# Multiplying half of the columns of the self-mirrored slots in a first dense layer, and computing the rest from sums and differences

## The chip, the cores and the metric

The kernel runs on one core of one Trainium2 chip. The metric is the device time of one execution, in microseconds; lower is better. Every time below is a median of several executions, with the lowest and highest in brackets. All executions that are compared were at a mean granted TensorE clock of 0.991 to 0.996 of full speed.

## The reference

```python
x: (8, 3008, 256)                      # fp32
X = fft(fft(x, axis=1), axis=2).real   # over the sequence, then over the width
x2 = X.reshape(24064, 256)
h = x2 @ w_in                          # w_in: 256 x 2048
g = h * clip(h + 3, 0, 6) / 6
return g @ w_out                       # w_out: 2048 x 256, fp32
```

## The kernel before

The transform over the sequence is done as 47 x 64: a token has the index k1 (47 values) and k2 (64 values). Batches go in 4 pairs. Of each pair there are 12 chunks of 4 slots; a slot is one batch with one k1 and all 64 k2, so a chunk has 256 columns. A chunk takes 8 steps, 384 in all. Because the input is real, the token at (k1, k2) and its mirror at (-k1, -k2) share their products: the first layer computes an even part `u` and an odd part `v`, a one-row correction gives `s`, and the two tokens are `s + v` and `s - v`. A slot with k1 = 0 is its own mirror. Such slots are the last two of the last chunk of each pair.

This is one step's first layer and activation (`ns` is 3 and `nm` is 2 in the last chunk, else both are 4; asserts and other cases cut):

```python
def mlp1(ch, fc):
    u = ps_h.tile([P, 2, KC, N2], F32, tag="uv")   # PSUM, one bank; u and v share 3 buffers
    v = ps_h.tile([P, 2, KC, N2], F32, tag="uv")
    for blk, ps in ((0, u), (1, v)):
        for i in range(2):
            matmul(ps[:, i], W1[r, blk, f*P:(f+1)*P], q[r, blk, of:of+KC])
    for i in range(2):                              # s = u + qn * WN, to SBUF
        vector.scalar_tensor_tensor(s[:, i], qn[...], WN[:, f:f+1], u[:, i], mult, add)
    vector.tensor_tensor(u[:, :, 0:ns], s[:, :, 0:ns], v[:, :, 0:ns], add)
    relu(t[:, 0, :, 0:ns], u[:, :, 0:ns], 1/6)      # ScalarE
    if ch.last:                                     # the negated sum
        vector.scalar_tensor_tensor(u[:, :, 3], s[:, :, 3], -1.0, v[:, :, 3], mult, subtract)
        relu(t[:, 0, :, 3], u[:, :, 3], -1/6)
    vector.tensor_tensor(v[:, :, 0:nm], v[:, :, 0:nm], s[:, :, 0:nm], subtract)
    relu(t[:, 1, :, 0:nm], v[:, :, 0:nm], -1/6)
    gate(a[:, 0, :, 0:ns], t[:, 0, :, 0:ns], u[:, :, 0:ns])   # VectorE: min(t, 1) * u
    if ch.last:
        gate(a[:, 1, :, 2], t[:, 0, :, 3], u[:, :, 3])
    for i in ...:
        gate(a[:, 1, i, 0:nm, ::-1], t[:, 1, i, 0:nm], v[:, i, 0:nm])
```

The steps run in this order. The first layer is two steps ahead of the second, GpSimd forms sums for the second layer one step ahead, and in the first three steps of a chunk the chunk before it is finished: GpSimd recombines it in step 0 and VectorE transposes it in steps 1 and 2.

```python
for s, (p, ck, fc) in enumerate(steps):
    if s + 2 < len(steps): mlp1(*chunk(s + 2))
    if s + 1 < len(steps): combine(*chunk(s + 1))     # GpSimd
    if prev and fc < 3:
        finish(prev) if fc == 0 else store(prev, fc - 1)
    mlp2(*chunk(s))            # 14 MATMULs: 7 products, Strassen-like
    ...
```

## Time and profile before

| | before |
|---|---|
| median of 3 runs | 2004.63 us (2003.18 to 2004.73) |
| span of the profiled run, granted clock | 2001.0 us, 0.993 |
| TensorE work of a step of the last chunk, by the prediction's sum | 4.01 us |
| what a step there takes, without and with transposes (pair 1) | 4.12 us, 4.68 and 4.69 us |
| first to seventh second-layer call of a last chunk, pairs 0, 1, 2 | 26.59, 25.94, 25.96 us |
| first to sixth, pair 3 | 21.82 us |

The lines of the profile are shown in the prediction. The last two rows of the table are the measure that I call "the stretch". It runs from the start of the first second-layer call of a last chunk to the start of the seventh; in pair 3, which has no next pair to begin, to the start of the sixth. It holds the five steps that the prediction calls bound by VectorE.

### The profile page before, as it was taken

The page shows a single profiled execution, that of the slowest core. Times are in us where ns is not written, and L with a number is a line of the kernel's source. Part 1 is how long each engine was busy: PE and PEld are TensorE (multiplying, and loading weights), DVE is VectorE, ACT ScalarE, POOL GpSimd, SP SyncE. Part 2 cuts the span into 40 slices and gives each one's busy share as a digit, 9 for nine tenths or more (in the row PEclk, how much of TensorE's full clock was granted, in tenths as well). Part 3 has the DMA queues.
Part 4 walks back from the last instruction along what each step waited for, and adds up shares of the span by engine and source line. Part 5 has one row for each costly group of instructions (what it writes and reads, how often), then busy time and mean ns, then how long its engine had stood idle before and what let it go on. Part 6 is the DMA issues. An engine that isn't in the chain of part 4 may idle for free.

```text
span 2001.0 us, 28370 instructions
## 1 busy us (share of the span) xinstructions
PE 1965.6 (98%) x9178; PEld 1691.6 (85%) x9178; DVE 1440.1 (72%) x2711; ACT 700.3 (35%) x1196; POOL 1416.2 (71%) x1608
## 2 busy tenths in 40 slices
PE   8899999999999999999999999999999999999997
PEld 5588888888888888888888888888888888888886
DVE  5677767776777677776777767777678777777776
ACT  6533333333333333333333333333333333333322
POOL 3277778776777787777658877778666667667664
PEclk9899999999999999999999999999999999999999
DMA  9512212211111122110201221212110101101100
GB/s 296 143 28 58 51 40 50 57 36 35 29 34 51 41 52 59 47 51 25 50 17 30 70 57 39 51 44 52 35 27 20 27 17 26 33 12 27 27 12 19
DMA packets 158665, 93.54 MB, mean 47 GB/s; under 512 B 130635, under 2 KB 143467, under 8 KB 158518
## 3 DMA queue, kind: packets, MB, share of 16 engines
q1 hardware_dynamic: 148310, 57.99, 12.0%
q0 software_dynamic: 9600, 33.59, 6.0%
q8 instruction: 75, 1.23, 0.2%
q14 instruction: 72, 0.59, 0.1%
q10 hardware_dynamic: 608, 0.13, 0.0%
HBM read 54.32 MB, written 37.33 MB: 46 GB/s over the span
## 4 chain that ended last, share of the span: by engine, by line
PE 93%; DVE 3%; ACT 1%; issue 1%; POOL 0%; DVEq 0%; POOLq 0%; ACTq 0%
PE acc L382 55%; PE v L326 16%; PE u L326 16%; PE ps L280 2%; PE ps L226 2%; DVE a L358 1%; ACT t L355 0%; DVE u L339 0%; DVE s L331 0%; DVE o L440 0%; ACT PM L498 0%; PE wps L563 0%; DVE v L345 0%; DVE u L342 0%; ACT q L282 0%
## 5 line engine op out<-in xcount | busy, mean ns | idle before, releaser
L372 POOL TENSOR_TENSOR c<-a 128x512 f32<-128x512 f32 (+1 forms) x383 | 478.2, 1249 | 452.3 <-PE acc L382 358.3
L382 PE MATMUL acc<-c,G 128*128 128x256 f32 (+1 forms) x3072 | 712.0, 375 | 0.0
L355 ACT ACTIVATE t<-u,half 128x512 f32<-128x512 f32 (+2 forms) x416 | 272.5, 655 | 1105.7 <-DVE u L339 1094.1
L382 PEld LDWEIGHTS acc<-c,G 128*128 128x128 f32 x3072 | 577.5, 190 | 72.8
L331 DVE SCALAR_TENSOR_TENSOR s<-qn,WN,u 128x256 f32<-128x256 f32 x768 | 334.2, 476 | 352.8 <-PE u L326 352.4
L382 PE MATMUL acc<-a,G 128*128 128x256 f32 (+1 forms) x2304 | 551.7, 375 | 0.0
L382 PEld LDWEIGHTS acc<-a,G 128*128 128x128 f32 x2304 | 434.9, 190 | 57.7
L326 PE MATMUL v<-q,W 127*128 127x256 f32 x1536 | 398.6, 381 | 7.6 <-DVE a L358 7.6
L326 PE MATMUL u<-q,W 128*128 128x256 f32 x1536 | 395.4, 380 | 1.8 <-DVE a L358 1.5
L326 PEld LDWEIGHTS u<-q,W 128*128 128x128 f32 x1536 | 287.8, 190 | 59.7 <-issue 15.6
L326 PEld LDWEIGHTS v<-q,W 127*128 127x128 f32 x1536 | 290.2, 190 | 55.7 <-issue 8.2
L358 DVE SCALAR_TENSOR_TENSOR a<-t,u 128x512 f32<-128x512 f32 (+2 forms) x416 | 265.9, 646 | 96.0 <-ACT t L355 90.0
L372 POOL TENSOR_TENSOR c<-c,a 128x256 f32<-128x256 f32 (+1 forms) x383 | 274.7, 717 | 30.0
L372 POOL TENSOR_TENSOR c<-a,c 128x256 f32<-128x256 f32 (+1 forms) x383 | 274.5, 717 | 30.0
L339 DVE TENSOR_TENSOR u<-s,v 128x512 f32<-128x512 f32 (+1 forms) x384 | 263.1, 685 | 42.1 <-PE v L326 1.6
L355 ACT ACTIVATE t<-v,half 128x512 f32<-128x512 f32 (+1 forms) x384 | 257.1, 670 | 5.8 <-DVE v L345 4.4
L345 DVE TENSOR_TENSOR v<-v,s 128x512 f32<-128x512 f32 (+1 forms) x384 | 257.7, 671 | 1.1
L358 DVE SCALAR_TENSOR_TENSOR a<-t,v 128x512 f32<-128x512 f32 (+1 forms) x416 | 254.9, 619 | 0.5
L372 POOL TENSOR_TENSOR r<-w,e 128x256 f32<-128x256 f32 (+1 forms) x94 | 90.8, 987 | 3.7
L390 ACT ACTIVATE e<-acc 128x512 f32<-128x512 f32 (+2 forms) x190 | 86.3, 544 | 2.8 <-PE acc L382 2.7
L440 DVE STREAM_TRANSPOSE o<-r 128x256 f32<-128x256 f32 (+1 forms) x192 | 72.5, 415 | 0.4
L238 ACT COPY z<-ps 96x512 f32<-96x512 f32 x64 | 37.2, 581 | 82.8 <-PE ps L226 62.5
(91 smaller groups left out, 755.7 us busy)
## 6 DMA issues: line engine op xcount, KB each, us to landing
out_dram<-o SPq DMA_DIRECT2D x732, 32.0 KB
zd<-z SPq DMA_DIRECT2D x32, 384.0 KB
g<-zd SPq DMA_DIRECT2D x48, 256.0 KB
xt<-in_x_dram POOLq DMA_DIRECT2D x21, 384.0 KB, 4.0
qn<-qd SPq DMA_DIRECT2D x23, 256.0 KB
st<-in_moe_w_in_dram POOLq DMA_DIRECT2D x8, 512.0 KB, 11.1
st<-in_moe_w_out_dram POOLq DMA_DIRECT2D x8, 512.0 KB, 5.0
xt<-in_x_dram POOLq DMA_DIRECT2D x7, 376.0 KB, 3.9
```

Source lines behind the costliest of these rows:

```text
L226: nc.tensor.matmul(ps[0:PZ], F[0:PR, 0:PZ], y[:, 2 * i:2 * i + 2, :], start=True, stop=True)
L280: nc.tensor.matmul(ps[:, blk, 2 * u:2 * u + 2], g[:, kk, blk * (P + 1):blk * (P + 1) + P], T[:, :, gr, blk, kk], start=True, stop=True)
L326: nc.tensor.matmul(ps[:, i], W1[r, blk, f * P:(f + 1) * P], q[r, blk, of:of + KC], start=True, stop=True)
L331: nc.vector.scalar_tensor_tensor(s[:, i].rearrange("p k n -> p (k n)"), qn[:, of * N2:(of + KC) * N2], WN[:, f:f + 1], u[:, i].rearrange(" ...
L339: nc.vector.tensor_tensor(u[:, :, 0:ns], s[:, :, 0:ns], v[:, :, 0:ns], op=AL.add)
L345: nc.vector.tensor_tensor(v[:, :, 0:nm], v[:, :, 0:nm], s[:, :, 0:nm], op=AL.subtract)
L355: nc.scalar.activation(t, h, AF.Relu, bias=half[:], scale=scale)
L358: nc.vector.scalar_tensor_tensor(dst, t, 1.0, h, op0=AL.min, op1=AL.mult)
L372: (eng or nc.gpsimd).tensor_tensor(out, in0, in1, op=AL.add)
L382: nc.tensor.matmul(ch.acc[i // 2][:, i % 2, 0:ch.n], G[:, i, fc, :], mv, start=(fc == 0 and i % 2 == 0), stop=(fc == NF - 1), skip_group_c ...
L390: nc.scalar.mul(ch.e[:, k:i + 1, 0:ch.n], ch.acc[i // 2][:, 0:i + 1 - k, 0:ch.n], 1.0 / WS)
L440: nc.vector.transpose(o[:, 0:n // DH, h], ch.r[:, m, h, 0:n].rearrange("p (j i) -> p j i", i=DH))
```

## The change

In a slot with k1 = 0, the even part is the same at k2 and at 64 - k2, and the odd part has the opposite sign. So products for k2 = 0 to 32 are enough (`NH` = 33): the last chunk has 128 + 66 = 194 columns to multiply in place of 256. The tokens k2 = 33 to 63 come from the same products with the signs exchanged. The intent is to save TensorE about a quarter of the first layer in 32 of the 384 steps. VectorE gets more and smaller instructions for it. The diff, cut to the first layer and the activation (the second transform stage also skips the 31 columns of both slots):

```diff
     def mlp1(ch, fc):
-                nc.tensor.matmul(ps[:, i], W1[r, blk, f * P:(f + 1) * P], q[r, blk, of:of + KC],
+                nc.tensor.matmul(ps[:, i, 0:nq], W1[r, blk, f * P:(f + 1) * P], q[r, blk, of:of + nq],
                                  start=True, stop=True)
...
+    def activate_last(a, t, s, u, v):
+        n, e2, e3 = 2 * N2, 2 * N2 + NH, 2 * N2 + 2 * NH      # 128, 161, 194
+        m = NH - 2                                            # 31
+        two, three = slice(n + 1, e2 - 1), slice(e2 + 1, e3 - 1)
+        mine, minus = slice(e2, e2 + m), slice(e2 + m, e3 + m)
+        nc.vector.tensor_tensor(u[:, :, 0:e2], s[:, :, 0:e2], v[:, :, 0:e2], op=AL.add)
+        nc.vector.tensor_tensor(u[:, :, mine], s[:, :, two], v[:, :, two], op=AL.subtract)
+        nc.vector.scalar_tensor_tensor(u[:, :, minus], s[:, :, e2:e3], -1.0, v[:, :, e2:e3],
+                                       op0=AL.mult, op1=AL.subtract)
+        relu(t[:, 0, :, 0:e2 + m], u[:, :, 0:e2 + m], 1.0 / 6.0)
+        relu(t[:, 0, :, minus], u[:, :, minus], -1.0 / 6.0)
+        nc.vector.tensor_tensor(v[:, :, 0:e3 - 1], v[:, :, 0:e3 - 1], s[:, :, 0:e3 - 1], op=AL.subtract)
+        relu(t[:, 1, :, 0:e3 - 1], v[:, :, 0:e3 - 1], -1.0 / 6.0)
+        back = slice(3 * N2 - 1, e2 - 1, -1)
+        gate(a[:, 0, :, 0:e2], t[:, 0, :, 0:e2], u[:, :, 0:e2])
+        gate(a[:, 0, :, back], t[:, 0, :, mine], u[:, :, mine])
+        gate(a[:, 1, :, n:e2], t[:, 0, :, minus], u[:, :, minus])
+        for i in range(2):
+            ...  gate(rev[:, :, ::-1], tk, vk)                # 2 x 128 elements, reversed
+        gate(a[:, 1, :, back], t[:, 1, :, three], v[:, :, three])
```

Besides the width, the order changes: the negated sum now comes before the first activation.

More of the change, by code (lines that the diff above doesn't have):

```diff
@@ L82 @@
     TB = KC * N2
+    NH = N2 // 2 + 1
     NG = NCK // 2
@@ L272, in stage2 @@
         if i == 0:
-            pr.q[gr] = qpool.tile([P, 2, 2 * KC, N2], F32, tag="q", name="q")
+            pr.q[gr] = qpool.tile([P, 2, 2 * TB], F32, tag="q", name="q")
         g = pr.g[gr]
-        ps = bank([P, 2, 4, N2], "ps2")
+        ps = bank([P, 2, TB], "ps2")
         for u in range(2):
             kk = 2 * i + u
+            nk = NH if (gr, kk) == (NG - 1, 2 * KK - 1) else N2
+            n = u * P + 2 * nk
             for blk in range(2):
-                nc.tensor.matmul(ps[:, blk, 2 * u:2 * u + 2], g[:, kk, blk * (P + 1):blk * (P + 1) + P],
-                                 T[:, :, gr, blk, kk], start=True, stop=True)
-        nc.scalar.copy(pr.q[gr][:, :, 4 * i:4 * i + 4, :], ps[:])
+                nc.tensor.matmul(ps[:, blk, u * P:n].rearrange("p (b k) -> p b k", b=2),
+                                 g[:, kk, blk * (P + 1):blk * (P + 1) + P],
+                                 T[:, :, gr, blk, kk, 0:nk], start=True, stop=True)
+        nc.scalar.copy(pr.q[gr][:, :, i * TB:i * TB + n], ps[:, :, 0:n])
     def spread(pr, gr):
@@ L293, in spread @@
         else:
+            n = 2 * TB if gr < NG - 1 else 3 * P + 2 * NH
             qd = dpool.tile([1, 2 * TB], F32, tag="qd", name="qd")
-            nc.sync.dma_start(out=qd[:], in_=pr.q[gr][P - 1:P, 1].rearrange("p k n -> p (k n)"))
-            nc.sync.dma_start(out=pr.qn[gr][:], in_=qd[:].to_broadcast([P, 2 * TB]))
+            nc.sync.dma_start(out=qd[:, 0:n], in_=pr.q[gr][P - 1:P, 1, 0:n])
+            nc.sync.dma_start(out=pr.qn[gr][:, 0:n], in_=qd[:, 0:n].to_broadcast([P, n]))
         del pr.g[gr]
@@ L306, in __init__ @@
             self.ns = 3 if self.last else KC
-            self.nm = 2 if self.last else KC
             self.n = self.ns * N2
+            self.nq = P + 2 * NH if self.last else TB
             self.a, self.c, self.acc = {}, {}, {}
@@ L316, in mlp1 @@
     def mlp1(ch, fc):
-        gr, of = ch.ck // 2, ch.ck % 2 * KC
+        gr, of, nq = ch.ck // 2, ch.ck % 2 * TB, ch.nq
         q, qn = ch.pr.q[gr], ch.pr.qn[gr]
-        u = ps_h.tile([P, 2, KC, N2], F32, tag="uv", name="u")
-        v = ps_h.tile([P, 2, KC, N2], F32, tag="uv", name="v")
+        u = ps_h.tile([P, 2, TB], F32, tag="uv", name="u")
+        v = ps_h.tile([P, 2, TB], F32, tag="uv", name="v")
         for blk, ps in ((0, u), (1, v)):
@@ L325, in mlp1 @@
                 f = fc + i * NF
-                nc.tensor.matmul(ps[:, i], W1[r, blk, f * P:(f + 1) * P], q[r, blk, of:of + KC],
+                nc.tensor.matmul(ps[:, i, 0:nq], W1[r, blk, f * P:(f + 1) * P], q[r, blk, of:of + nq],
                                  start=True, stop=True)
-        s = spool.tile([P, 2, KC, N2], F32, tag="s", name="s")
+        s = spool.tile([P, 2, TB], F32, tag="s", name="s")
         for i in range(2):
             f = fc + i * NF
-            nc.vector.scalar_tensor_tensor(
-                s[:, i].rearrange("p k n -> p (k n)"), qn[:, of * N2:(of + KC) * N2], WN[:, f:f + 1],
-                u[:, i].rearrange("p k n -> p (k n)"), op0=AL.mult, op1=AL.add)
@@ L336, in mlp1 @@
-        ns, nm = ch.ns, ch.nm
-        a = apool.tile([P, 2, 2, KC, N2], F32, tag="a", name="a")
-        t = spool.tile([P, 2, 2, KC, N2], F32, tag="t", name="t")
-        nc.vector.tensor_tensor(u[:, :, 0:ns], s[:, :, 0:ns], v[:, :, 0:ns], op=AL.add)
-        relu(t[:, 0, :, 0:ns], u[:, :, 0:ns], 1.0 / 6.0)
-        if ch.last:
-            nc.vector.scalar_tensor_tensor(u[:, :, 3], s[:, :, 3], -1.0, v[:, :, 3],
-                                           op0=AL.mult, op1=AL.subtract)
-            relu(t[:, 0, :, 3], u[:, :, 3], -1.0 / 6.0)
@@ L345, in mlp1 @@
-        nc.vector.tensor_tensor(v[:, :, 0:nm], v[:, :, 0:nm], s[:, :, 0:nm], op=AL.subtract)
-        relu(t[:, 1, :, 0:nm], v[:, :, 0:nm], -1.0 / 6.0)
-        gate(a[:, 0, :, 0:ns], t[:, 0, :, 0:ns], u[:, :, 0:ns])
-        if ch.last:
-            gate(a[:, 1, :, 2], t[:, 0, :, 3], u[:, :, 3])
-        for i in (slice(0, 2),) if nm == KC else (0, 1):
-            gate(a[:, 1, i, 0:nm, ::-1], t[:, 1, i, 0:nm], v[:, i, 0:nm])
-        ch.a[fc] = a
+            nc.vector.scalar_tensor_tensor(s[:, i, 0:nq], qn[:, of:of + nq], WN[:, f:f + 1], u[:, i, 0:nq],
+                                           op0=AL.mult, op1=AL.add)
@@ new lines, in mlp1 @@
+        a = apool.tile([P, 2, 2, TB], F32, tag="a", name="a")
+        t = spool.tile([P, 2, 2, TB], F32, tag="t", name="t")
+        ch.a[fc] = a
+        if ch.last:
+            activate_last(a, t, s, u, v)
+            return
+        nc.vector.tensor_tensor(u[:], s[:], v[:], op=AL.add)
+        relu(t[:, 0], u[:], 1.0 / 6.0)
+        nc.vector.tensor_tensor(v[:], v[:], s[:], op=AL.subtract)
+        relu(t[:, 1], v[:], -1.0 / 6.0)
+        gate(a[:, 0], t[:, 0], u[:])
+        rev, tk, vk = (m.rearrange("p i (k n) -> p (i k) n", n=N2) for m in (a[:, 1], t[:, 1], v[:]))
@@ new lines, in mlp1 @@
+        gate(rev[:, :, ::-1], tk, vk)
+    def activate_last(a, t, s, u, v):
[16 more added lines that the diff above has]
+        for i in range(2):
+            rev, tk, vk = (x.rearrange("p (k n) -> p k n", n=N2) for x in (a[:, 1, i, 0:n], t[:, 1, i, 0:n], v[:, i, 0:n]))
+            gate(rev[:, :, ::-1], tk, vk)
+        gate(a[:, 1, :, back], t[:, 1, :, three], v[:, :, three])
@@ L360, in combine @@
     def combine(ch, fc):
-        a = ch.a[fc][:].rearrange("p m f k n -> p (m f) (k n)")[:, :, 0:ch.n]
+        a = ch.a[fc][:].rearrange("p m f n -> p (m f) n")[:, :, 0:ch.n]
         c = cpool.tile([P, 4, TB], F32, tag="c", name="c")
@@ L374, in mlp2 @@
     def mlp2(ch, fc):
-        a = ch.a.pop(fc)[:].rearrange("p m f k n -> p (m f) (k n)")[:, :, 0:ch.n]
+        a = ch.a.pop(fc)[:].rearrange("p m f n -> p (m f) n")[:, :, 0:ch.n]
         c = ch.c.pop(fc)
```

## The prediction

> **What bounds the kernel now.** I read the page from the top: busy shares, then the chain that ended last, then the groups by shape, and last the timeline of one stretch. The page says:
>
> ```profile
> PE 1965.6 (98%) x9178; PEld 1691.6 (85%) x9178; DVE 1440.1 (72%) x2711; ACT 700.3 (35%) x1196; POOL 1416.2 (71%) x1608
> ...
> PE 93%; DVE 3%; ACT 1%; issue 1%; POOL 0%; DVEq 0%; POOLq 0%; ACTq 0%
> ```
>
> TensorE is the bound nearly everywhere: 93% of the chain. But the change touches only the last of the 12 chunks of each of the 4 pairs of batches, 8 steps each, 32 of 384 steps, so the average does not answer; that chunk has to be read by itself. A step is one first-layer call (8 MATMULs, two for each of four products), the activation on VectorE and ScalarE, the sums on GpSimd, and one second-layer call (14 MATMULs). The first-layer call runs two steps ahead. TensorE in pair 1's last chunk, timeline (start, duration):
>
> ```profile
> 1036.19 1.10 PE L326 MATMUL v<-q,W 127*128 127x256 f32 x4 [0.44 <-DVE a L358]
> 1037.13 1.14 PE L382 MATMUL acc<-a,G 128*128 128x192 f32 x6
> 1038.10 1.46 PE L382 MATMUL acc<-c,G 128*128 128x192 f32 x8
> 1039.40 1.03 PE L326 MATMUL u<-q,W 128*128 128x256 f32 x4
> 1040.31 1.10 PE L326 MATMUL v<-q,W 127*128 127x256 f32 x4
> ```
>
> The step lasts 1040.31 - 1036.19 = 4.12 us. TensorE's own work is less: the chain has 14 second-layer MATMULs of 192 columns in 2.28 us (162.8 ns each) and elsewhere 14 of 256 in 3.02 us (216 ns), so a step needs 8 x 216 + 2.28 = 4.01 us. In front of the v product it waits for the gate (the line `a`, L358). VectorE, then ScalarE, in the same step:
>
> ```profile
> 1036.36 0.86 DVE L331 SCALAR_TENSOR_TENSOR s<-qn,WN,u 128x256 f32<-128x256 f32 x2
> 1037.33 0.56 DVE L339 TENSOR_TENSOR u<-s,v 128x384 f32<-128x384 f32 x1
> 1038.60 0.30 DVE L342 SCALAR_TENSOR_TENSOR u<-s,v 128x128 f32<-128x128 f32 x1 [0.71 <-ACT t L355]
> 1038.93 0.43 DVE L345 TENSOR_TENSOR v<-v,s 128x256 f32<-128x256 f32 x1
> 1039.41 0.75 DVE L358 SCALAR_TENSOR_TENSOR a<-t,u 128x384 f32<-128x384 f32 x2
> 1040.08 0.48 DVE L358 SCALAR_TENSOR_TENSOR a<-t,v 128x128 f32<-128x128 f32 x2
> 1040.47 0.48 DVE L331 SCALAR_TENSOR_TENSOR s<-qn,WN,u 128x256 f32<-128x256 f32 x1
> ```
>
> ```profile
> 1037.98 0.58 ACT L355 ACTIVATE t<-u,half 128x384 f32<-128x384 f32 x1 [2.09 <-DVE u L339]
> 1038.93 0.37 ACT L355 ACTIVATE t<-u,half 128x128 f32<-128x128 f32 x1 [0.36 <-DVE u L342]
> 1039.46 0.47 ACT L355 ACTIVATE t<-v,half 128x256 f32<-128x256 f32 x1 [0.16 <-DVE v L345]
> ```
>
> VectorE starts the next step's `s` 4.11 us after this one and has no gap above 0.11 us in between but the 0.71 us in which L342 waits for ScalarE. So this chunk is bound by the serial run of VectorE, wait included. A second loop is as long: u and v share three PSUM buffers, so the v product of a step starts only when the u gates of the step before are done (1040.16, the product starts 1040.31). In two steps of each last chunk VectorE also transposes the chunk before (0.76 us for two), and these last 4.68 and 4.69 us (v product to v product, 1026.82, 1031.50, 1036.19). From the first second-layer call of pair 1's last chunk (1019.42) to the seventh (1045.36) pass 25.94 us; TensorE alone would need 6 x 4.01 = 24.06.
>
> Durations for the estimates, by shape (after the count: total us, mean ns; then idle time before them and what ended it):
>
> ```profile
> L358 DVE SCALAR_TENSOR_TENSOR a<-t,u 128x384 f32<-128x384 f32 x32 | 17.7, 554 | 1.8 <-POOL w L400 0.4 <-ACT t L355 0.4
> ...
> L358 DVE SCALAR_TENSOR_TENSOR a<-t,v 128x128 f32<-128x128 f32 x64 | 15.2, 279 | 0.0
> ...
> L355 ACT ACTIVATE t<-u,half 128x128 f32<-128x128 f32 x32 | 11.8, 368 | 11.6 <-DVE u L342 11.6
> ...
> L342 DVE SCALAR_TENSOR_TENSOR u<-s,v 128x128 f32<-128x128 f32 x32 | 9.5, 296 | 22.9 <-ACT t L355 22.9
> ```
>
> VectorE costs (554 - 279)/256 = 1.07 ns per element and some 140 ns fixed; a following instruction that waits for nothing starts about 0.08 us before the end (the 384 and 128 wide gates take 0.75 together, not 0.83).
>
> **What the Trainium skill says.** "PSUM — Partial Sum Buffer", Terms: two engines on one bank and quadrant at once are a collision error. u fills one bank (2 x 256 fp32), so VectorE and ScalarE must take turns on it. The trace agrees: L342 writes columns that the activation before it does not read, and waits all the same, 0.71 us here, 22.9 us over 32 steps. "VectorE: DVE Perf Modes", the TRN2 errata: each instruction pays a fixed cost, largest in proportion for small operands; the trace agrees with its 140 ns. "TensorE: Matmul & The Clock Gate", Wait — 56ns, not 53.3ns?: a warm stream is spaced by columns over 2.4 GHz plus some 2.5 ns. With two passes in each fp32 MATMUL this gives 216 ns for 256 columns, which is what the trace has. "ScalarE: Activation LUTs", What ACT_TABLE_LOAD costs: 0.833 ns per element, and back-to-back activations overlap by about 93 ns. The trace has (581 - 368)/256 = 0.832 (581 is the 384 wide activation's mean), and in ordinary chunks two activations of 0.69 us start 0.60 us apart (525.72 and 526.32).
>
> **The change, part by part.** NH is 33, so the first layer of the last chunk multiplies 128 + 66 = 194 columns for 256; the second layer keeps its 192.
>
> TensorE: a MATMUL of 194 takes 162.8 + 2 x 0.83 = 164.5 ns, so a step saves 8 x 51.5 = 0.41 us and would need 3.60 us. Over 32 steps that is 13.2 us. One of 16 products of the second transform stage per pair shrinks from 128 to 66 columns: 4 MATMULs of 62 columns less at 0.83 ns, 0.2 us per pair.
>
> VectorE, from the `s` of a step to the next: before, 9 instructions of 2048 elements; after, 12 of about 1990 (2 x 194, 322, 62, 66, 386, 322, 62, 66, 2 x 128, 62). The elements barely fall, three small instructions come on top, some 0.13 us of spacing each. Against this stands a reordering: all three writes of u now come before the first activation, and the subtraction for v fills the time in which ScalarE works, so L342's wait of 0.71 us goes. In its place the gates wait until both activations of u are over, since they read the same bank. Step by step, estimates from the durations above: `s` 0.97 - 0.13 = 0.84; u add 0.42, mirrored difference 0.15, negated sum 0.23 and 0.09 to ScalarE; its two activations 0.49 + 0.32, and 0.05 back; three u gates 0.41 + 0.13 + 0.13; three v gates 0.20 + 0.20 + 0.13. The sum is 0.84 + 1.75 + 0.67 + 0.52 (without rounding) = 3.78 us. Each place where I let one instruction run into the next may instead wait (L345 starts 0.03 us after L342 ends, not before), 0.11 us each in two or three places: up to 4.1. I take 3.85, for 4.11 before.
>
> ScalarE and GpSimd change by less than 0.05 us per step.
>
> What reaches the end: the first three of the eight first-layer calls stand beside second-layer calls of 256 columns, where TensorE is the bound (4.75 us per step): they save the whole 0.41, 1.24 us. The other five follow VectorE: 5 x (4.11 - 3.85) = 1.3, and the last u gates are done 0.3 us sooner, 1.6. With 0.2 from the transform stage, 3.05 us per pair, some 12 for four, a little less in the last pair, which has no next pair to start. 2004.6 - 12 is about 1992.5 us.
>
> **Rivals.** First, TensorE stays the bound throughout: if VectorE's run were under 3.60 us and the transposes found slack, 25.94 would fall to 5 x 3.60 + 4.01 = 22.0 us, 5.4 us per pair in all, 1983 us. The 72% of VectorE over the span speaks for it; the stretch above, where it has no slack, speaks against. Second, small instructions cost more than I allow: at 4.1 us the five steps give nothing but the 0.3 us, 1.7 per pair, 1998; at 4.3 it would be a wash near 2001. For it speaks the gap after L342; against it the 0.20 us spacing of the 128 wide gates. Third, GpSimd takes over: after a chunk ends it has the recombination of some 4.7 us between two sums, and in pair 1 the sums for the third step end at 1027.73, while the product that needs them starts at 1028.73. One microsecond of slack, which steps shorter by 0.3 to 0.4 us use up: it can take back about 0.3 us per pair, not more.
>
> **Range and chances.** The middle of VectorE's 3.78 to 4.1 gives 1992.5; the ends, with GpSimd's part and room for a lucky overlap, 1986.5 to 1998.5. All the rivals lie within 2% (40 us): even removing every stall cannot reach it, and a loss of 40 us would need 1.25 us more in each of 32 steps.
>
> **What would show it.** First-layer MATMULs in the last chunk 164.5 ns apart; the wait of the negated sum for ScalarE gone, and a wait of 0.3 to 0.5 us of the first u gate for the second activation in its place; `s` to `s` near 3.85 us where nothing is transposed; 1.24 us less in the three steps before. I am wrong if the five steps run at TensorE's 3.60 us, or if `s` to `s` is above 4.1.

## The result, and the profile after

After: 1998.83 us (1996.67 to 2000.36, 4 runs). Before, in the same rounds: 2003.91 us (2002.18 to 2004.73, 4 runs). The ratio is 0.9975, with a 95% interval of 0.9958 to 0.9992. Ratios are computed from the mean time of one kernel's fast runs over the mean of the other's in the same rounds, so they are not quite the ratios of the medians that I quote. The change gains 5.1 us by the medians; the prediction said 12, and the measured time lies 0.33 us above its range. A second measurement (e8 below) gives 6.4 us.

The page of the changed kernel, busy shares and then the chain that ended last, by engine:

```profile
PE 1954.7 (98%) x9178; PEld 1686.3 (84%) x9178; DVE 1447.1 (72%) x2807; ACT 694.6 (35%) x1196; POOL 1415.8 (71%) x1608
...
PE 90%; DVE 4%; ACT 1%; issue 1%; DMA 0%; SPq 0%; DVEq 0%; POOL 0%; POOLq 0%; ACTq 0%
```

TensorE is busy for 10.9 us less, VectorE for 7.0 us more, in 96 more instructions (3 in each of 32 steps). In the chain TensorE falls from 93% to 90% and VectorE rises from 3% to 4%: TensorE's saved time was largely turned into waiting. The spans themselves, 2001.0 and 1998.6 us, must not be compared at this scale. Pair 0's last chunk begins its second layer at 539.77 us in the profile before, at 542.25 us after and at 538.24 us in e8, which is the same kernel: 4 us between two runs of one kernel.

The groups by shape, TensorE, say where the waiting is (after the count: total us, mean ns; then the idle time before them and what ended it):

```profile
L333 PE MATMUL v<-q,W 127*128 127x194 f32 x128 | 27.8, 339 | 9.7 <-DVE a L384 9.7
L333 PE MATMUL u<-q,W 128*128 128x194 f32 x128 | 26.2, 328 | 0.0
```

All narrow products together wait 9.7 us, and always for the gate `a`. (The mean of one MATMUL, 328 ns, counts its overlap with the next; in a stream without waits, four of them take 0.66 us to the start of what follows, 1009.63 to 1010.29, which is the predicted 164.5 ns each.) TensorE's timeline in pair 1's last chunk, the step that the prediction shows of before:

```profile
1036.49 0.90 PE L333 MATMUL v<-q,W 127*128 127x194 f32 x4 [0.80 <-DVE a L384]
...
1039.50 0.82 PE L333 MATMUL u<-q,W 128*128 128x194 f32 x4
1040.55 0.90 PE L333 MATMUL v<-q,W 127*128 127x194 f32 x4 [0.23 <-DVE a L384]
```

The step takes 1040.55 - 1036.49 = 4.06 us, where before it took 4.12. A wait for the gate stands in front of the v products here, since u and v share their buffers. VectorE in the same step:

```profile
1036.79 0.73 DVE L338 SCALAR_TENSOR_TENSOR s<-qn,WN,u 128x194 f32<-128x194 f32 x2
1037.63 0.50 DVE L363 TENSOR_TENSOR u<-s,v 128x322 f32<-128x322 f32 x1
1038.16 0.23 DVE L364 TENSOR_TENSOR u<-s,v 128x62 f32<-128x62 f32 x1
1038.42 0.23 DVE L365 SCALAR_TENSOR_TENSOR u<-s,v 128x66 f32<-128x66 f32 x1
1038.69 0.57 DVE L369 TENSOR_TENSOR v<-v,s 128x386 f32<-128x386 f32 x1
1039.65 0.76 DVE L384 SCALAR_TENSOR_TENSOR a<-t,u 128x322 f32<-128x322 f32 x3 [0.39 <-ACT t L381]
1040.32 0.61 DVE L384 SCALAR_TENSOR_TENSOR a<-t,v 128x128 f32<-128x128 f32 x3
1040.85 0.73 DVE L338 SCALAR_TENSOR_TENSOR s<-qn,WN,u 128x194 f32<-128x194 f32 x2
```

From `s` to `s` pass 1040.85 - 1036.79 = 4.06 us. L364 starts 0.03 us after L363 has ended, and L365 0.03 us after L364; there is no overlap. The first gate then waits 0.39 us for ScalarE:

```profile
1038.75 0.79 ACT L381 ACTIVATE t<-u,half 128x384 f32<-128x384 f32 x2 [2.71 <-DVE u L365]
1039.43 0.59 ACT L381 ACTIVATE t<-v,half 128x386 f32<-128x386 f32 x1
```

ScalarE cannot start before the last of the three writes of u (L365, over at 1038.65), and no u gate starts before both activations of u are over (1039.54).

In the stretch of pair 1, TensorE's busy time fell from 25.05 to 23.39 us and VectorE's rose from 20.68 us in 59 instructions to 22.23 us in 77. The stretch itself: 25.95, 26.03 and 26.03 us in pairs 0 to 2, 21.42 us in pair 3. Against before that is -0.64, +0.09, +0.07 and -0.40, together -0.9 us. In the three steps ahead of the stretch, where TensorE is the bound, a step that took 4.76 us takes 4.34: two of them in pair 1 fell from 10.40 to 9.58 us, transform work between them included.

### The profile page after: what moved, and what is told of

The parts are those of the page before. It is cut to its first block, busy times and chain, and to the rows that moved or that the text cites. A ratio compares the mean times of both kernels' runs of the same rounds, so it can differ in the third digit from the quotient of the medians.

```text
span 1998.6 us, 27836 instructions
## 1 busy us (share of the span) xinstructions
PE 1954.7 (98%) x9178; PEld 1686.3 (84%) x9178; DVE 1447.1 (72%) x2807; ACT 694.6 (35%) x1196; POOL 1415.8 (71%) x1608
## 4 chain that ended last, share of the span: by engine, by line
PE 90%; DVE 4%; ACT 1%; issue 1%; DMA 0%; SPq 0%; DVEq 0%; POOL 0%; POOLq 0%; ACTq 0%
PE acc L408 54%; PE v L333 16%; PE u L333 15%; PE ps L227 2%; PE ps L284 2%; DVE a L384 1%; ACT t L381 1%; DVE s L338 1%; DVE u L363 0%; ACT PM L524 0%; DVE o L466 0%; PE wps L589 0%; DVE u L365 0%; DVE u L364 0%; PE ps L224 0%
## 5 line engine op out<-in xcount | busy, mean ns | idle before, releaser
L381 ACT ACTIVATE t<-u,half 128x512 f32<-128x512 f32 (+2 forms) x416 | 267.5, 651 | 1108.0 <-DVE u L348 1018.2
L338 DVE SCALAR_TENSOR_TENSOR s<-qn,WN,u 128x256 f32<-128x256 f32 (+1 forms) x768 | 330.0, 471 | 348.4 <-PE u L333 347.8
L333 PE MATMUL v<-q,W 127*128 127x256 f32 (+1 forms) x1536 | 391.0, 376 | 13.4 <-DVE a L384 13.4
L333 PE MATMUL u<-q,W 128*128 128x256 f32 (+1 forms) x1536 | 388.1, 375 | 2.4 <-DVE a L384 2.1
L384 DVE SCALAR_TENSOR_TENSOR a<-t,u 128x512 f32<-128x512 f32 (+3 forms) x448 | 266.1, 606 | 106.0 <-ACT t L381 103.0
L348 DVE TENSOR_TENSOR u<-s,v 128x512 f32<-128x512 f32 x352 | 245.0, 696 | 38.1 <-DVE s L338 0.9
L384 DVE SCALAR_TENSOR_TENSOR a<-t,v 128x512 f32<-128x512 f32 (+2 forms) x448 | 258.9, 590 | 0.5
L350 DVE TENSOR_TENSOR v<-v,s 128x512 f32<-128x512 f32 x352 | 243.7, 692 | 0.0
```

The lines of the kernel that those rows point to most:

```text
L333: nc.tensor.matmul(ps[:, i, 0:nq], W1[r, blk, f * P:(f + 1) * P], q[r, blk, of:of + nq], start=True, stop=True)
L338: nc.vector.scalar_tensor_tensor(s[:, i, 0:nq], qn[:, of:of + nq], WN[:, f:f + 1], u[:, i, 0:nq], op0=AL.mult, op1=AL.add)
L348: nc.vector.tensor_tensor(u[:], s[:], v[:], op=AL.add)
L350: nc.vector.tensor_tensor(v[:], v[:], s[:], op=AL.subtract)
L381: nc.scalar.activation(t, h, AF.Relu, bias=half[:], scale=scale)
L384: nc.vector.scalar_tensor_tensor(dst, t, 1.0, h, op0=AL.min, op1=AL.mult)
```

## The experiments

My theory was that VectorE's serial run, with the waits inside it, bounds these five steps, and that the run shrank less than I had summed because instructions wait for each other where I had let them overlap. The rivals: the small instructions cost more in themselves, wherever they write; the loop of the three u/v buffers holds the step; GpSimd's sums hold it; and the narrow products, not the order of the activation, bring what was gained. The expectations below use a letter for a theory; S is mine, and a letter other than S stands for a rival.

Ten kernels ran; nine returned the right result, and e2 is wrong. e1 to e4 ran on one chip in 5 rounds (before: 2005.77 us), e5 to e8 on another in 5 rounds (before: 2003.24 us), e9 and e10 on a third in 3 rounds (before: 2004.3 us).

| run | median (range, n), us | ratio to before, 95% | stretch pair 0 / 1 / 2 / 3, us |
|---|---|---|---|
| e1_wide | 2004.91 (2001.69–2007.15, 5) | 0.9995 (0.9981–1.0008) | 25.91 / 25.98 / 25.98 / 21.54 |
| e2_six_plain | 1982.76 (1981.34–1984.12, 4) | 0.9885 (0.987–0.9901) | 21.99 / 21.97 / 21.97 / 17.97 |
| e3_late_store | 1994.65 (1991.3–1995.82, 5) | 0.9942 (0.9929–0.9956) | 24.81 / 24.53 / 24.53 / 21.42 |
| e4_reorder | 2001.97 (2000.29–2004.19, 5) | 0.9985 (0.9971–0.9999) | 25.97 / 25.35 / 25.36 / 21.25 |
| e5_sbuf_mirror | 1987.83 (1985.91–1989.26, 5) | 0.9923 (0.9909–0.9937) | 23.27 / 23.26 / 23.60 / 19.27 |
| e6_sbuf_mirror_late | 1983.86 (1981.45–1986.73, 4) | 0.9905 (0.989–0.9921) | 22.19 / 22.19 / 22.19 / 19.27 |
| e7_before_sbuf | 1994.47 (1993.9–1997.09, 5) | 0.996 (0.9946–0.9973) | 24.20 / 24.04 / 24.04 / 20.03 |
| e8_after_again | 1996.86 (1995.0–2000.41, 5) | 0.9972 (0.9958–0.9985) | 25.97 / 26.05 / 26.04 / 21.43 |
| e9_self_waits_only | 1996.17 (1991.91–1998.7, 4) | 0.9949 (0.9925–0.9974) | 24.96 / 25.32 / 25.32 / 20.90 |
| e10_negated_in_v | 1992.68 (1992.48–1996.92, 4) | 0.994 (0.9918–0.9962) | 24.47 / 24.82 / 24.82 / 20.36 |

### e1: the wide products put back, VectorE as changed

```diff
-                nc.tensor.matmul(ps[:, i, 0:nq], W1[r, blk, f * P:(f + 1) * P], q[r, blk, of:of + nq],
+                nc.tensor.matmul(ps[:, i], W1[r, blk, f * P:(f + 1) * P], q[r, blk, of:of + TB],
```

(The transform stage fills the 62 missing columns again, so that no product reads what was not written.)

> The changed kernel with its products wide again (256 columns, the extra 62 unused; result right), VectorE as in the changed kernel. Theory S (VectorE's serial run sets the five steps of the last chunk): from the first to the seventh second-layer call of pair 1's last chunk still 26.0 us, `s` to `s` still 4.06; only the three steps before lose 0.41 us each and the transform stage 0.2 to 0.3 per pair, together 1.5 x 4 = 6 us more than the changed kernel, some 2004.5, equal to the kernel before within 1.5. Rival P (TensorE's narrower products shorten all eight steps): 13 us more than the changed kernel, 2012, and 28 us or more in that stretch.

The time is that of before. The stretch is as long as after the change, 25.98 us in pair 1, with steps of 4.08 us where the change has 4.05. So narrowing the products does nothing for the five steps: it is worth the rest, some 1.5 us per pair in the three steps ahead and in the transform stage. A qualification: with wide products a step of this kernel is also about as long as the u/v buffer loop (v products at 1035.06 and 1039.71 in a step with a transpose, each released by the gates), so this run alone does not separate the run of VectorE from the loop through it.

### e2: six plain VectorE instructions in place of twelve (result wrong)

The narrow products stay, and `s` keeps its two instructions; the ten that follow become four over 192 columns each, with nearly as many elements. The mirrored tokens are not formed, so the result is wrong (relative error 0.22).

```diff
+        nc.vector.tensor_tensor(u[:, :, 0:n3], s[:, :, 0:n3], v[:, :, 0:n3], op=AL.add)
+        relu(t[:, 0, :, 0:n3], u[:, :, 0:n3], 1.0 / 6.0)
+        nc.vector.tensor_tensor(v[:, :, 0:n3], v[:, :, 0:n3], s[:, :, 0:n3], op=AL.subtract)
+        relu(t[:, 1, :, 0:n3], v[:, :, 0:n3], -1.0 / 6.0)
+        gate(a[:, 0, :, 0:n3], t[:, 0, :, 0:n3], u[:, :, 0:n3])
+        gate(a[:, 1, :, 0:n3], t[:, 1, :, 0:n3], v[:, :, 0:n3])
```

> The changed kernel with 6 VectorE instructions per step of the last chunk in place of 12, elements nearly the same (1930 for 1990), no instruction there waiting for VectorE itself but the first sum; narrow products kept; result wrong on purpose. Theory S: VectorE needs some 3.1 us per step, TensorE's 3.6 becomes the bound, the stretch of six steps goes from 26.0 to 22.0 to 22.4, the time to 1983 to 1986. Rival G (GpSimd or the u/v buffers set the five steps): stretch above 25, time above 1995.

TensorE's timeline of this kernel, from one u product to the next:

```profile
1028.22 0.82 PE L333 MATMUL u<-q,W 128*128 128x194 f32 x4
...
1031.81 0.82 PE L333 MATMUL u<-q,W 128*128 128x194 f32 x4
```

No bracket stands behind a line: TensorE waits for nothing. The steps are 3.59 us, which is its own work by the prediction's sum (3.60), and the stretch is 21.97 us for a predicted floor of 22.0. The transposes, the u/v buffers and GpSimd are all still there. So VectorE's run, with its waits, was the whole bound; neither the number of buffers nor GpSimd sets a floor above 3.60. It is also about the most that narrower products could have given: 23 us against the kernel before (2005.77 - 1982.76).

### e3: the transposes moved out of the last chunk

```diff
+            if ck == NCK - 1 and p < NP - 1:
+                held = prev
+            else:
+                store(prev, fc - 1)
+        if held and ck == 0 and fc in (3, 4):
+            store(held, fc - 3)
```

> The changed kernel with the four transposes moved out of the last chunk into the next pair's first chunk, for pairs 0 to 2; result right. Theory S: the two long steps (4.63) become 4.06, 1.15 us less in the stretch (24.9), 3.4 us less in all, 1995.4. Rival B (the three shared u/v buffers set the pace, transposes lie beside): no change.

The stretch falls from 26.03 to 24.53 us, 1.5 in place of the expected 1.15 us: both steps of 4.63 become 4.06, and the last step loses a stall of 0.36 us (it is taken up under "The sum over the stretch"). Pair 3, whose transposes stay, keeps 21.42. What is on VectorE in these steps counts, whatever it is for.

### e4: the kernel before, with only the order changed

```diff
-        relu(t[:, 0, :, 0:ns], u[:, :, 0:ns], 1.0 / 6.0)
         if ch.last:
             nc.vector.scalar_tensor_tensor(u[:, :, 3], s[:, :, 3], -1.0, v[:, :, 3],
                                            op0=AL.mult, op1=AL.subtract)
+        relu(t[:, 0, :, 0:ns], u[:, :, 0:ns], 1.0 / 6.0)
+        if ch.last:
             relu(t[:, 0, :, 3], u[:, :, 3], -1.0 / 6.0)
```

> The kernel before with one line moved: the negated sum before the first activation, as in the changed kernel; all widths as before; result right. Theory S: the 0.71 us wait goes, a wait of the sum for the sum before (0.1) and of the gate for the second activation come; u sum to gate from 2.08 to 1.92, `s` to `s` 3.95 for 4.11, 0.8 to 1.0 us per pair, 3 to 4 us in all, about 2000.5. That would be most of what the changed kernel gains in the five steps. Rival: the reordering gives nothing by itself, 2004.

Steps without transposes now run at 4.01 us, TensorE's own work at 256 columns, and those with transposes at 4.56. The stretches are 0.6 us shorter in each pair (0.8 to 1.0 was expected), 2.4 us in all, which is more than the whole change gains in them (0.9 us). The gain that the change has in the five steps is thus one of order, and its three extra instructions take back a part of it.

### e5: the two mirrored sums in SBUF, not in u's bank

```diff
+        tu, tv, hm, hn, tm, tn = part      # six pieces of the tile t, in SBUF
         nc.vector.tensor_tensor(u[:, :, 0:e2], s[:, :, 0:e2], v[:, :, 0:e2], op=AL.add)
-        nc.vector.tensor_tensor(u[:, :, mine], s[:, :, two], v[:, :, two], op=AL.subtract)
-        nc.vector.scalar_tensor_tensor(u[:, :, minus], s[:, :, e2:e3], -1.0, v[:, :, e2:e3],
-                                       op0=AL.mult, op1=AL.subtract)
-        relu(t[:, 0, :, 0:e2 + m], u[:, :, 0:e2 + m], 1.0 / 6.0)
-        relu(t[:, 0, :, minus], u[:, :, minus], -1.0 / 6.0)
+        relu(tu, u[:, :, 0:e2], 1.0 / 6.0)
+        nc.vector.tensor_tensor(hm, s[:, :, two], v[:, :, two], op=AL.subtract)
+        nc.vector.scalar_tensor_tensor(hn, s[:, :, e2:e3], -1.0, v[:, :, e2:e3], op0=AL.mult, op1=AL.subtract)
+        relu(tm, hm, 1.0 / 6.0)
+        relu(tn, hn, -1.0 / 6.0)
```

The same instructions with the same elements; only the place of two results differs, and with it what waits for what. The list of the program's instructions says so (L363 to L384 are of the changed kernel, L369 to L375 of this one):

```text
L363 TensorTensor    u<-s,v 128x2x161   waits DVE_49, PE_49
L364 TensorTensor    u<-s,v 128x2x31    waits DVE_49
L365 TensorScalarPtr u<-s,v 128x2x33    waits DVE_49
L384 TensorScalarPtr a<-t,u 128x2x161   waits Activation_49, Pool_49

L369 TensorTensor    u<-s,v 128x2x161   waits DVE_49, PE_49
L371 TensorTensor    t<-s,v 128x62      no wait
L372 TensorScalarPtr t<-s,v 128x66      no wait
L375 TensorTensor    v<-v,s 128x2x193   waits DVE_49
```

In the changed kernel each write of u waits on VectorE's own semaphore, that is, until the one before it has finished. The trace agrees: L364 and L365 start 0.02 us after this semaphore was set by the write before them, and in e5 L371 and L372 wait for no semaphore. That it is the wait that counts, and not the place of the result, can be seen in ordinary chunks: there the write of v (L350) has no such wait and starts some 0.09 us before the write of u (L348) is over, in all 352 cases, and both write PSUM.

> The changed kernel with the mirrored difference and the negated sum written to SBUF (free room of the t tile) instead of into u's PSUM bank, with their own two small activations; same 12 VectorE instructions of the same sizes; result right. Theory S with its cause (writes to one bank wait for each other, and the gates of u wait for the second activation of that bank): these waits go, VectorE's run falls from 4.06 to some 3.5 us, below TensorE's 3.6; steps 3.6 us but for the two with transposes (4.0 to 4.2), stretch 22.2 to 22.8 us for 26.0, 20 us below the kernel before (ratio 0.990). Rival N (twelve instructions cost too much whatever they wait for): run still 3.9 or more, stretch above 25, ratio 0.997.

VectorE's timeline of this kernel, one step:

```profile
1030.42 0.73 DVE L338 SCALAR_TENSOR_TENSOR s<-qn,WN,u 128x194 f32<-128x194 f32 x2
1031.26 0.50 DVE L369 TENSOR_TENSOR u<-s,v 128x322 f32<-128x322 f32 x1
1031.66 0.21 DVE L371 TENSOR_TENSOR t<-s,v 128x62 f32<-128x62 f32 x1
1031.79 0.22 DVE L372 SCALAR_TENSOR_TENSOR t<-s,v 128x66 f32<-128x66 f32 x1
1032.04 0.57 DVE L375 TENSOR_TENSOR v<-v,s 128x386 f32<-128x386 f32 x1
1032.52 0.48 DVE L390 SCALAR_TENSOR_TENSOR a<-t,u 128x322 f32<-128x322 f32 x1
```

L371 starts 0.40 us after L369, before that one is over, and L372 0.13 us after L371; in the changed kernel these were 0.53 and 0.26 us. The gate waits for nothing, since ScalarE could start on u right after L369. The next `s` starts at 1033.89, so `s` to `s` is 3.47 us. That is the theory's number, and it rules out that the small instructions are dear in themselves: there are just as many here. Steps run at TensorE's 3.59 us where nothing else interferes.

The stretch, 23.26 us, is longer than the 22.2 to 22.8 that I had expected. VectorE, and then GpSimd, at the place where it is lost:

```profile
1020.46 1.27 DVE L390 SCALAR_TENSOR_TENSOR a<-t 128x62 f32<-128x62 f32 x2
```

```profile
1018.73 1.96 POOL L404 TENSOR_TENSOR r<-w,e 128x256 f32<-128x256 f32 x2
1020.65 1.01 POOL L404 TENSOR_TENSOR c<-a 128x384 f32<-128x384 f32 x1
```

Two small gates, which now read both inputs from SBUF, take 1.27 us where the same two take 0.35 in other steps; they end (1021.73) just after GpSimd's sum (1021.66). The median of such a gate is 221 ns, the longest 1042. The step made late by it takes 4.36 us. This is no chance meeting. Of the 64 such gates of this kernel 12 took over 0.26 us, and every one of them ends 0.08 us after an instruction of GpSimd does; e6 and e9 have 15 and 8 more, all at 0.08 to 0.09 us. So the move out of PSUM has a price: a gate with both operands in SBUF can be held up by GpSimd.

### e6: e5 with the transposes moved as in e3

```diff
+        if held and ck == 0 and fc in (3, 4):
+            store(held, fc - 3)      # with the rest of e3's edit
```

> The same with the transposes moved out of the last chunk as in e3. Theory S: TensorE bound, steps 3.6 us, stretch 22.0 us, 21 to 22 us below the kernel before (ratio 0.989). Rival N: as e3 or little better, ratio 0.994.

The stretches of pairs 0 to 2 are 22.19 us, 0.2 above TensorE's floor, and the steps 3.59 to 3.70. This is the fastest correct kernel: 19.4 us below the kernel before (21 to 22 was expected) and 13.0 us below the changed kernel of the same rounds (1983.86 / 1996.86 = 0.9935).

### e7: the kernel before, with its one negated sum in SBUF

```diff
-            nc.vector.scalar_tensor_tensor(u[:, :, 3], s[:, :, 3], -1.0, v[:, :, 3],
-                                           op0=AL.mult, op1=AL.subtract)
-            relu(t[:, 0, :, 3], u[:, :, 3], -1.0 / 6.0)
+        nc.vector.scalar_tensor_tensor(hn[:, :, 0], s[:, :, 3], -1.0, v[:, :, 3], op0=AL.mult, op1=AL.subtract)
+        relu(tn[:, :, 0], hn[:, :, 0], -1.0 / 6.0)
```

> The kernel before, all 256 columns multiplied, with its one negated sum written to SBUF instead of u's bank; result right. Theory S: the 0.71 us wait goes, VectorE's run 3.3 to 3.4 us, TensorE's 4.01 binds, also in steps with transposes; stretch 24.1 us for 25.94, 7.5 to 8 us below the kernel before (ratio 0.996), more than the change gains, without multiplying less. Rival N: no more than the reordering gave, 2001.5 to 2003, ratio 0.9985.

All 256 columns are multiplied, and all steps, those with transposes too, run at TensorE's 4.00 to 4.01 us. The stretch is 24.04 us for a floor of 24.06. The kernel gains 8.8 us against before, and its median is 2.4 us below that of the changed kernel on the same chip (their intervals against before overlap, so I do not call it faster). By the medians, taking one wait away was worth at least as much as multiplying a quarter less. The small gate whose inputs are both in SBUF costs 431 ns on the mean here, against 279 for one of its size that reads PSUM, and this time it fits.

### e8: the changed kernel again, beside e5 to e7

> The changed kernel as it is, beside the others on the same chip: ratio 0.9975 to the kernel before, stretch 26.0 us. Both theories expect the same; it serves to compare.

The ratio, 0.9972, agrees with the first one, 0.9975. The stretches agree to 0.02 us. So they are properties of the program and can be compared between kernels to a few hundredths, unlike the times.

### e9: the waits of VectorE on itself taken away, the gate's wait kept

The mirrored sums are in SBUF as in e5, but u's main activation comes after the two small ones again, so the first gate waits for ScalarE as in the changed kernel. Against e5:

```diff
         nc.vector.tensor_tensor(u[:, :, 0:e2], s[:, :, 0:e2], v[:, :, 0:e2], op=AL.add)
-        relu(tu, u[:, :, 0:e2], 1.0 / 6.0)
         ...
         relu(tm, hm, 1.0 / 6.0)
         relu(tn, hn, -1.0 / 6.0)
+        relu(tu, u[:, :, 0:e2], 1.0 / 6.0)
```

> As e5 (mirrored values in SBUF, so no instruction of VectorE waits for another over u's bank), but the two small activations put before the large one, so the gates of u again wait for ScalarE's whole queue, as in the changed kernel. This keeps the gates' wait and takes away the writes' waits. If the writes' waits are the term I mis-sized, `s` to `s` falls to my own estimate of 3.78 us (3.7 to 3.85), sum of u to first gate 1.75 for 2.02, stretch 24.1 to 24.6 us, ratio to the kernel before 0.994. If they cost nothing, 4.0 or more and a stretch near 26.

VectorE's timeline in a step without transposes, from the sum into u to the first gate:

```profile
1034.49 0.50 DVE L369 TENSOR_TENSOR u<-s,v 128x322 f32<-128x322 f32 x1
1034.90 0.21 DVE L370 TENSOR_TENSOR t<-s,v 128x62 f32<-128x62 f32 x1
1035.03 0.22 DVE L371 SCALAR_TENSOR_TENSOR t<-s,v 128x66 f32<-128x66 f32 x1
...
1036.32 0.49 DVE L390 SCALAR_TENSOR_TENSOR a<-t,u 128x322 f32<-128x322 f32 x1 [0.47 <-POOL c L404]
```

The three sums follow each other after 0.41 and 0.13 us, as in e5; in the changed kernel it was 0.53 and 0.26. The first gate still waits for the activations. (The bracket names GpSimd, whose sum was over 0.02 us later than ScalarE's activation; in two other steps of this chunk the bracket of this gate names ScalarE, with the same 0.47.)

| | sum into u to first gate, us | `s` to `s`, us |
|---|---|---|
| step without transposes: changed kernel, e9 | 2.02, 1.83 | 4.06, 3.87 |
| step just after the transposes: changed kernel, e9 | 1.95, 1.75 | 3.94, 3.75 |
| the prediction | 1.75 | 3.78 |

So in like steps `s` to `s` falls by 0.19 us, most of the 0.28 by which the prediction's sum was short; 3.87 is just above the 3.7 to 3.85 that I had expected. The run is not a clean removal of the waits, since ScalarE has three activations for u in place of two: they begin 0.40 us sooner after the sum into u, and take 1.00 us in place of 0.79. What it shows directly is the two spacings. The stretch missed what I expected of it, 25.32 us for 24.1 to 24.6: it contains the 0.36 us stall, and small gates on SBUF were held up in two steps (two of them took 0.61 and 0.83 us at 1019.36 and 1023.49, for 0.36 in other steps).

### e10: the negated sum into v's bank

```diff
-        nc.vector.scalar_tensor_tensor(u[:, :, minus], s[:, :, e2:e3], -1.0, v[:, :, e2:e3],
+        nc.vector.scalar_tensor_tensor(v[:, :, minus], s[:, :, e2:e3], -1.0, v[:, :, e2:e3],
                                        op0=AL.mult, op1=AL.subtract)
-        relu(t[:, 0, :, minus], u[:, :, minus], -1.0 / 6.0)
...
-        relu(t[:, 1, :, 0:e3 - 1], v[:, :, 0:e3 - 1], -1.0 / 6.0)
+        relu(t[:, 1, :, 0:e3 + NH], v[:, :, 0:e3 + NH], -1.0 / 6.0)
```

> The changed kernel with the negated sum written into free columns of v's bank and its activation joined to v's, so u's bank has one activation; the writes to the banks still wait for each other; result right. Expected from the durations: first gate of u at 1.67 us after the sum (VectorE's own chain of writes then sets it) for 2.02, but the v gates come to wait for a longer activation of v; `s` to `s` 3.9 to 4.0, stretch 25 to 25.6, ratio 0.996. If the second activation of u were the whole loss, 3.7 and a stretch of 24.2.

Nothing goes to SBUF and one activation is saved, and the first gate comes 1.55 us after the sum into u (1032.66 to 1034.21), 0.47 us sooner than in the changed kernel. Two thirds of this is lost further on, where the v gates now wait 0.23 us for a longer activation of v: `s` to `s` is 3.91 us, 0.15 less than in the changed kernel. It is a middle course, 24.82 us in pair 1 (25 to 25.6 was expected, and the first gate at 1.67 us), without the risk from GpSimd.

## Why the prediction was right and wrong

**What bounds the kernel now: right.** The last chunk was bound by VectorE's serial run, wait included. e2 confirms it from the other side: with a short run the steps drop to TensorE's own 3.60 us and stay there.

**TensorE's saving: right.** The narrow products follow each other as predicted, and the three steps ahead of the stretch save 0.41 to 0.42 us each. Two side remarks of the prediction are off without harm: its formula for a stream of 256 columns, with two passes, gives 218 ns and not the 216 that it names and the trace has; and the 4 MATMULs that shrink per pair are 2 products of 48, not one of 16. With the transform stage the prediction had 1.45 us per pair, 5.8 us in all. e1, which lacks just this, gives back nearly the whole measured gain.

**The wait of the negated sum: right.** L342's wait is gone, and the 0.39 us wait of the first gate for ScalarE stands in its place, within the predicted 0.3 to 0.5.

**The step that failed: the sum that the prediction works out "Step by step".** It took "u add 0.42, mirrored difference 0.15", as if each instruction could run into the next. They measured 0.53 and 0.26, because all three write u and each waits for the one before it to finish. These two terms make up 0.22 of the 0.27 us by which the piece from the sum into u to the first gate was too short (2.02 for 1.75). The other pieces held: `s` 0.84 as predicted, the u gates 0.67 as predicted, the v gates 0.53 for 0.52. The prediction named the possibility ("up to 4.1") and then took 3.85; 4.06 is near the top. (It calls 1992.5 us the middle of 3.78 to 4.1, but the middle is 3.94, which its own sum turns into some 1994.) The evidence was among its own lines: L345 began 0.03 us after L342's end, where gates that wait for nothing begin 0.08 us before it.

**The last gates: wrong.** "The last u gates are done 0.3 us sooner" was 0.05 us by the accounting below. With a u piece of 2.02 us there was nothing left of it.

**The sum over the stretch.** In pair 1 it is the time to the first sum into u, five runs of VectorE, the way from the sixth such sum to the release of the next v product, and 0.94 us of that product up to the second-layer call:

| | to first sum | five runs | sum to v product | rest | stretch |
|---|---|---|---|---|---|
| before | 0.31 | 21.72 | 2.97 | 0.94 | 25.94 |
| after | 0.39 | 21.78 | 2.92 | 0.94 | 26.03 |

Five runs of VectorE, two of them with transposes, should have been five times 0.05 us shorter. They contain a stall instead: the sum into u starts at 1042.04, though `s` was over at 1041.58 and the v product at 1041.45, where the usual gap is 0.10 us. That is 0.36 us.

The profile names no releaser, and no run was made for it, but the traces show where such stalls stand. Count all the instructions that the trace records on VectorE, those of its sequencer too: the late sum in pair 1 is number 1984. The same number 1984 is late by as much in e1, e5, e8, e9 and e10. In pair 2 it is number 2880, in the third step. In pair 0 it is ScalarE that stalls in the third step: its number 576, an activation of u, starts 0.33 us after the instruction before it, where 0.05 is usual. All these numbers are 64 more than a multiple of 128. In the twelve traces VectorE stands idle for 0.385 to 0.42 us before 142 instructions; 100 of them have such a number, whatever they do, and 32 of the others are e9's gates that wait for ScalarE. After each of the 100, within 0.65 to 1.64 us, a packet of 8192 bytes begins on DMA queue 14, which the page calls "instruction". e3, which moves instructions, moves the stall out of the stretches of pairs 1 and 2. So the stall goes with a place in the engine's own stream of instructions, not with operands or waits. Not every such place has it, and that the loading of instructions brings it about, as the packets suggest, is not shown: **its cause stays open.**

The kernel before has two such stalls in pair 0 (VectorE's number 960 and ScalarE's 576, 0.62 us together), the changed kernel three, 1.0 us together. Without them the five steps would have gained about 1.25 us and not 0.9, an estimate from these figures; that is 0.4 of the 5.5 us that they lack against the prediction (6.4 less 0.9). The main finding, which e5 and e9 show in steps without it, doesn't rest on it.

**The balance.** The prediction had 5.8 us outside the five steps and 6.4 us (4 times 1.6) in them. The profiles have 5.8 and 0.9, together 6.7; measured are 5.1 and, in e8, 6.4. So the direction and the mechanism were right, and one term of the sum was mis-sized by 0.2 to 0.3 us in each step, which cost about half of the gain.

**The rivals.** Its second rival, small instructions that cost more than allowed, came nearest in the numbers (1998 us at a run of 4.1), but for a different reason: not their cost (e5 has as many), but what they wait for. The first rival, TensorE as the bound throughout at 1983 us, was a possible world and not this kernel: e2 and e6 reach it at 1982.76 and 1983.86 us. Of the third rival, GpSimd, I found nothing in the changed kernel; it shows in e5 and e9, once operands lie in SBUF.

What no run tried is a fourth buffer for u and v. (The kernel's three PSUM pools hold 1, 3 and 4 buffers of one bank each.)

## What to carry to other kernels

When an engine writes several small results into one PSUM bank, look in the instruction list for waits on the engine's own semaphore, and sum such instructions without overlap; moving a result that needn't be there to another place can be worth more than the arithmetic that a change saves. Work saved on the engine that leads the average is gained only in the stretches where it leads; read these separately, and take the other stretches' serial run wait by wait. Before moving an operand to SBUF for this, see whether GpSimd is running at the time.

## What the Trainium skill lacked or had wrong

- "VectorE: DVE Perf Modes", The DRAIN you can't avoid, says of chained instructions that "the semaphore costs nothing extra here". Its example is eight equal copies. For the small instructions of this kernel the trace differs: with a wait on VectorE's own semaphore the next one starts 0.53 and 0.26 us after its predecessor, without it 0.40 and 0.13 us (the changed kernel against e5). The wait cost 0.13 us each time. The section does say that an instruction which is not held starts earlier, but gives no number for it.
- "SBUF — State Buffer", Terms, describes the port pair that VectorE and GpSimd share as a lock, where the loser is blocked. The trace agrees in kind: two small gates with both inputs in SBUF took 1.27 us in place of 0.35 while GpSimd's sum ran. What the entry lacks is how this shows for small instructions: a median of 221 ns and a longest of 1042 ns for the same gate in e5, and an end 0.08 to 0.09 us after that of GpSimd's instruction for all 35 late ones of e5, e6 and e9.
- No page gives a stall at fixed places of an engine's stream of instructions (it would belong to "Runtime: NRT & Kernel Launch", Instruction fetch mechanics). Here VectorE is idle for some 0.40 us, and ScalarE for 0.33, before recorded instructions whose number is 64 more than a multiple of 128: 100 times on VectorE in twelve traces.
